# A kernel of two attention layers and two convolutions: the end of the second attention core in halves, fewer row transfers, and other orders of steps

## The chip, the cores and the metric

The kernel runs on one core of a Trainium2 chip. A core has five engines with queues of their own that work in order and meet at semaphores: PE (TensorE, matmul), DVE (VectorE), ACT (ScalarE), POOL (GpSimd) and SP, which here issues most of the DMA transfers. The metric is device time in microseconds (us) of one launch. The median of three runs is compared; a profile of one more execution tells where its time goes.

## The reference, cut to what matters

The input `x` has 2048 rows of 512. Four layers are added to it in turn: A, B, A, B, each on the layer-normalised `x`; both A layers share their weights, and so do both B layers.

```python
def _A_ref(x, wqkv, wo):            # H = 32 heads of 16, window W = 8, dilation 2
    qkv = split_heads(x @ wqkv); q, k, v = qkv[0], qkv[1], qkv[2]
    idx = pos[:, None] - off[None, :]          # off = 0, 2, ..., 14; masked where idx < 0
    logits = einsum("bhsd,bhswd->bhsw", q, kg) * scale
    attn = softmax(logits)
    o = einsum("bhsw,bhswd->bhsd", attn, vg)
    return merge_heads(o) @ wo

def _B_ref(u, ...):                 # K[d, l] = Re sum_n C P dB: a filter of 2048 taps for each channel
    y = irfft(rfft(pad(u)) * rfft(pad(K)))[:L].astype(bfloat16)
    return y + u * Dskip

x = x + _A_ref(_layernorm(x), A_wqkv, A_wo)
x = x + _B_ref(_layernorm(x), ...)
x = x + _A_ref(_layernorm(x), A_wqkv, A_wo)
x = x + _B_ref(_layernorm(x), ...)
```

## The kernel before

Everything stays on one core. `x` lies in SBUF as `x_sb`, 128 partitions by 16 "rows" (row `a` of partition `p` is token `16p + a`) by 512 channels. No scheduler orders the work: each part is a string of one-letter or short steps (`ORDERK`, `CORE0`, `ORDER0`, `ORDERF`, `CORE1`, `ORDER1`), and the engines get their instructions in the order in which the steps stand there. A step issues instructions on several engines at once: a matmul group on PE and its copy out of PSUM on ACT or DVE, for instance. So moving a step in a string moves it in every queue that it uses.

The parts in order of time:

- `k_gen` (`ORDERK`) makes the filters `K`, normalises `x`, and projects the first layer's `k` and part of `q`. It does not change.
- `LayerA.core` (`CORE0`, later `CORE1`) is the attention. `m` multiplies `q` by shifted `k` (DVE, tile `prod`), `l` sums over channels (PE, tile `L` in PSUM), `x`, `e`, `r`, `n`, `T` are the softmax; `P` multiplies attention by shifted `v` for one row (DVE, tile `pav`); `S` (or `V`, with wider matmuls) sums that over the window on PE into `po` and copies it to `oT` (ACT); `O` projects `oT` with `wo` (PE, into a tile `pq` that `p` has filled with the old `x` where it stands ahead) and copies the result to `x_sb` (ACT). `a` and `f` normalise a finished row into `u` for the convolution on DVE and ACT; `b` and `d` begin and end the statistics of a block of four rows. The last row (15) is multiplied in two halves of 256 channels, so that PE can start on the first.
- In `CORE0` more steps are woven in: `1` and `6` load the two halves of the filter rows (`k_load`), `A` to `H` permute them, `W` to `Z` and `2` to `5` make a table of sines, `w` loads a quarter of the table `w_sb`.
- `FftB.run` (`ORDER0`, `ORDER1`) is the convolution through a two-step Fourier transform, for two halves of the channels: `K` and `U` transform filter and input (first step; the letter A or D behind says whether ACT or DVE copies out), `k` and `u` the second step, `m` multiplies spectra (DVE), `y` or `Y` (wider matmuls) is the first inverse step, `w`, `v` and `z` the second one with the addition into `x_sb` for eight rows of 128 channels, four rows of 128, or four rows of 256. In the first convolution each result of `k` is also exchanged between neighbouring partitions by transfers, and stored for the second convolution, which loads it back.
- `ORDERF` is the passage from the first convolution into the second attention: `h`, `H`, `a`, `p`, `n` are statistics, root and normalised rows of four rows at a time, `T` the transposes on PE, `E` their copies out, `P` and `Q` the projections of `k` and `q` (PE, copied by ACT), `x` shifted copies of `k`.

The lines that the argument uses: L342 (`m` of the core), L467 (`P`), L492 and L482 (`S`, `V`), L494 (copy to `oT`), L509 (`O` on PE), L514 (its copy to `x_sb`), L138 (row statistics), L155 and L156 (root as logarithm and exponential on ACT), L195 and L197 (a normalised row on ACT, on DVE or POOL), L811 (copies out of the Fourier steps), L822 (first step on PE), L868 (`m` of the convolution), L880 (copy of `u`), L943 and L944 (second inverse step), L946 and L948 (its addition on DVE, its copy on ACT), L1425 (row transfers of `k_load`), L599 (loads of `w_sb`).

After the string `CORE1` the core's end is written out as plain calls: statistics of rows 12 to 14, projection of row 15, eight matmuls whose result nobody reads, statistics of row 15, and the normalised rows 12, 13 (DVE), 14 (ACT) and 15 (DVE).

## Time and profile before

| what | us |
|---|---|
| median of 3 runs (lowest, highest) | 398.29 (397.69, 398.57) |
| the profiled execution's own time | 398.55 |
| its span, first to last instruction | 396.7 |
| busy in the span: DVE | 377.6 |
| busy in the span: PE (matmul) | 345.0 |
| busy in the span: ACT | 333.1 |
| busy in the span: POOL | 43.3 |

The 1.85 us between the profiled execution's time and its span lie ahead of the first instruction and behind the last. An engine that is busy for most of a stretch sets its length; idle time of another engine in that stretch costs nothing. A row of a timeline has start, duration (of all its instructions, where several are merged), engine, line, operation, tiles and shapes, the count, and in brackets the idle time of the engine before it with what ended it. Durations of neighbouring rows overlap by about 0.1 us. Granted clock of the core over the span: 0.976; it is 1.00 in every stretch from 107 us to 381 us.

### The profile page before, as it was taken

Reading aid. Unit: us, or ns where it says so; the run is one execution under the profiler, and the core shown is the slowest. Engines: PE = TensorE matmul, PEld = TensorE weight load, DVE = VectorE, ACT = ScalarE, POOL = GpSimd, SP = SyncE. Lnnn points to the kernel's source line nnn. Section 1 sums busy time; section 2 is a strip of 40 time slices with the busy share of each in tenths; the row PEclk is TensorE's granted clock in tenths of the full one; section 3 lists DMA queues with packets and bytes.
Section 4 is the critical chain, followed back from the end, with each engine's and each line's share of the span. In section 5 each row is a group of like instructions: output and inputs, shape, how many; then the busy total and the mean of one; then the engine's idle time right before and its main releaser. Section 6 shows DMA issues by size and latency. Waiting matters only on the chain.

```text
span 396.7 us, 14893 instructions
## 1 busy us (share of the span) xinstructions
PE 345.0 (87%) x6509; PEld 236.4 (60%) x6556; DVE 377.6 (95%) x453; ACT 333.1 (84%) x594; POOL 43.3 (11%) x93
## 2 busy tenths in 40 slices
PE   3865768799999999899997879999999998887895
PEld 2221236485645677666886878543456676566885
DVE  6999999999999999999999899979999999989995
ACT  7999999999568789989999987675566889989974
POOL 9400100000370001002422200100000001000000
PEclk9996599999999999999999999999999999999999
DMA  7953610313215756395563744820153029504507
GB/s 215 396 158 47 72 55 10 85 29 79 65 48 143 192 156 192 98 327 208 178 234 130 286 141 111 293 81 0 34 167 93 5 90 338 162 4 144 179 5 214
DMA packets 63695, 54.18 MB, mean 137 GB/s; under 512 B 33033, under 2 KB 49966, under 8 KB 63374
## 3 DMA queue, kind: packets, MB, share of 16 engines
q1 hardware_dynamic: 61958, 48.70, 41.2%
q0 software_dynamic: 1664, 4.52, 3.1%
q8 instruction: 51, 0.84, 0.8%
q14 instruction: 14, 0.11, 0.2%
q10 hardware_dynamic: 8, 0.00, 0.0%
HBM read 30.15 MB, written 13.24 MB: 109 GB/s over the span
## 4 chain that ended last, share of the span: by engine, by line
PE 37%; DVE 27%; ACT 20%; DMA 8%; issue 6%; SPq 1%; POOL 1%; DVEq 0%; ACTq 0%; POOLq 0%
DVE pav L467 7%; PE pq L398 6%; ACT a1s L811 5%; PE pq L223 4%; PE pk L1320 4%; PE pp L282 3%; DVE t L868 3%; DVE prod L342 3%; DMA w_sb<-w_dram 3%; PE pp L1258 2%; PE po L492 2%; ACT ub L880 2%; PE L L350 2%; DVE A_t L1154 2%; DVE ln_bn L138 2%
## 5 line engine op out<-in xcount | busy, mean ns | idle before, releaser
L467 DVE TENSOR_TENSOR pav<-attn,v_ext 128x4096 bf16<-128x4096 bf16 (+1 forms) x34 | 72.0, 2158 | 0.3
L342 DVE TENSOR_TENSOR prod<-qT,kT_ext 128x4096 bf16<-128x4096 bf16 x29 | 65.2, 2283 | 0.7 <-PE L L350 0.5
L1154 DVE TENSOR_TENSOR A_t<-A_t,pow_t 128x1024 bf16<-128x1024 bf16 (+4 forms) x46 | 38.0, 871 | 0.4
L492 PEld LDWEIGHTS <-pav 64*128 64x128 bf16 x1664 | 26.4, 95 | 13.6 <-DVE pav L467 7.1
L880 ACT CAST ub<-pb 128x1024 bf16<-128x1024 f32 x32 | 31.9, 1088 | 2.2 <-DVE t L868 1.2
L509 PE MATMUL pq<-wop,oT 128*128 128x512 bf16 x113 | 30.9, 380 | 3.0 <-issue 1.5
L492 PE MATMUL po<-ident,pav 64*128 64x64 bf16 x1664 | 28.9, 190 | 4.3 <-ACT oT L484 1.8
L829 PE MATMUL pb<-a1s,w_sb 128*128 128x64 bf16 x768 | 27.6, 193 | 5.5 <-ACT ub L880 1.9
L398 PE MATMUL pq<-wv,xnT 128*128 128x512 bf16 x122 | 29.8, 379 | 0.2
L829 PEld LDWEIGHTS <-w_sb 128*128 128x128 bf16 x768 | 24.8, 98 | 8.0 <-issue 6.2
L811 ACT CAST a1s<-pb 128x1024 bf16<-128x1024 f32 x29 | 28.1, 1061 | 1.1 <-PE pb L822 1.1
L400 ACT CAST v_ext<-pq 128x512 bf16<-128x512 f32 x32 | 18.7, 587 | 12.0 <-PE pq L398 11.9
L1258 PE MATMUL pp<-xnT,kT_ext 128*128 128x512 bf16 x88 | 23.0, 379 | 6.3 <-ACT xnT L1251 3.1
L225 ACT CAST qT<-pq 128x512 bf16<-128x512 f32 x24 | 14.0, 585 | 12.8 <-PE pq L223 12.8
L1320 PE MATMUL pk<-B_t,A_t 128*64 128x84 bf16 (+1 forms) x512 | 23.4, 201 | 0.9 <-ACT kgs L1328 0.8
L1320 PEld LDWEIGHTS <-A_t 128*64 128x64 bf16 (+1 forms) x512 | 21.5, 103 | 4.3 <-issue 1.4
L811 DVE CAST a1s<-pb 128x1024 bf16<-128x1024 f32 x19 | 22.5, 1213 | 1.4 <-PE pb L822 1.3
L223 PE MATMUL pq<-xnT,kT_ext 128*128 128x512 bf16 x89 | 23.4, 380 | 0.4
L1122 PE MATMUL pt<-ws,ident 128*128 128x512 f32 x16 | 11.8, 830 | 11.5 <-ACT ws L1109 11.5
L398 PEld LDWEIGHTS <-xnT 128*128 128x128 bf16 x128 | 11.7, 98 | 13.6 <-issue 1.3
L509 PEld LDWEIGHTS <-oT 128*128 128x128 bf16 x128 | 11.5, 98 | 13.1 <-ACT oT L494 2.2
L822 PE MATMUL pb<-F1c,xnT 128*64 128x128 bf16 x256 | 17.3, 219 | 1.6 <-ACT a1s L811 0.6
(279 smaller groups left out, 901.6 us busy)
## 6 DMA issues: line engine op xcount, KB each, us to landing
w_sb<-w_dram SPq DMA_DIRECT2D x32, 256.0 KB, 5.4
w_dram<-xnT SPq DMA_DIRECT2D x1, 4096.0 KB
kf_ring<-kf_dram SPq DMA_DIRECT2D x13, 256.0 KB, 3.9
kf_ring<-kf_dram SPq DMA_DIRECT2D x26, 128.0 KB, 3.5
v_ext<-v_ext SPq DMA_DIRECT2D x4, 784.0 KB, 6.2
x_blk<-in_A_x_dram SPq DMA_DIRECT2D x4, 512.0 KB, 4.7
kT_ext<-in_A_wqkv_dram SPq DMA_DIRECT2D x4, 512.0 KB, 9.7
x_sb<-in_A_x_dram SPq DMA_DIRECT2D x4, 512.0 KB, 7.0
```

Of the source, the lines that this page charges most:

```text
L223: nc.tensor.matmul(pq[:], lhsT=self.wqk[:, dt, ft * P:(ft + 1) * P], rhs=self.xnT[:, dt, q * 512:(q + 1) * 512], start=(dt == 0), stop=(dt ...
L342: nc.vector.tensor_tensor(pr, self.qT[q][:, ft].unsqueeze(1).to_broadcast([P, W, 4, P]), kap, ALU.mult)
L398: nc.tensor.matmul(pp[:], lhsT=xnT[:, dt, a * P:(a + 1) * P], rhs=wv[:, dt, :], start=(dt == 0), stop=(dt == NDT - 1))
L467: nc.vector.tensor_tensor(pv[:, i], attn[:, n % 4].unsqueeze(2).to_broadcast([P, W, DH // parts, H]), vap, ALU.mult)
L492: nc.tensor.matmul(po[:, h, 0, i * nt + ft, :], lhsT=pvf[rows, i, w, ft * P:(ft + 1) * P], rhs=ident[rows, rows], start=(w == 0 and ft + i ...
L509: nc.tensor.matmul(pw[:], lhsT=oT[:, ftp, :], rhs=self.wo[:, ftp, :], start=False, stop=(ftp == NDT - 1), skip_group_check=ahead)
L811: (self.nc.scalar.copy if eng == "act" else self.nc.vector.tensor_copy)(dst, src)
L829: nc.tensor.matmul(p2[:, j, :], lhsT=self.w2[:, ec * EC + j, :], rhs=a1s[:, ec * EC + j, :], start=True, stop=True)
L880: nc.scalar.copy(ub[:], p2)
L1154: return lambda: nc.vector.tensor_tensor(*args)
L1258: nc.tensor.matmul(pps[kind, b, ft][:], lhsT=la.wqk[:, dt, c:c + P], rhs=la.xnT[:, dt, b * 512:(b + 1) * 512], start=(dt == 0), stop=(dt = ...
L1320: nc.tensor.matmul(o, lhsT=lhs, rhs=Bt[:, ri, c * CH + ql].rearrange("p b g -> p (b g)"), start=(not half and j % 4 == 0 and ri == 0), sto ...
```

## The change

Four things are done together.

1. `k_load`: the block of 16 partitions, whose rows repeat with a period, is loaded by four transfers of four rows each instead of nine of one to three rows. This is so for each half of the channels. The bytes written are the same.
2. The end of the second core becomes steps of its string, `A` to `M`: row 15 is summed, copied and projected in two halves (`S` and `K`, then `L` and `M`), the second half in a bank of the tile `L`; the statistics of row 15 (`B`) follow directly; its normalised row (`I`) is taken out of PSUM (`pws[r]`), and its copy to `x_sb` (`D`) comes behind it on ACT. Row 13 is normalised by ACT (`G`) instead of DVE. The eight unread matmuls (`J`) come behind the projection.
3. The strings `CORE0`, `ORDER0`, `ORDERF`, `CORE1` and `ORDER1` are other orders of (nearly) the same steps. In `CORE0` and `CORE1` the letters are the same but for those of item 2; the first 107 letters of `CORE1` are unchanged.
4. In these strings a few copies change engine or width: in `ORDER0` one `UD` becomes `UA`; in `ORDERF` `E20D` becomes `E20A` and `v100A` becomes `v100D`; in `ORDER1` `w011D` becomes `v013A` and `v012D`, `v110A` becomes `v110D`, and one `yA` becomes `YA`.

```diff
 ORDER0 = """
-KD a q KA c3 c1 t s KA KA KD KA g r KD e c2 KA KD KA c6 c0 c5A KD c7 kA kD c4D KA kA kD KA KD UA KD
-UA UA UD KA UD UA UD UA kA kD kA kD u UD u UA UA m UD u u m m u u UA m m u u kD UA UA m m UA kD kA
-kD m u u u kD kD kA kA m m m yA u u YA yD m yA m u u u yA YA yA m m m w000D yD yA YD yA YA yD yA
-w010D
+a KD s t q KA KA KA KD KA c3 KD KA g c2 KD KA r e c0 KD KA c1 c5A c6 c4D c7 kA kD KA KD UA KD UA UA
+UD KA UD UA UD UA kA kD kA kD kA kD u u u m m u kD UA kD m m kA UA UA u UD u u kD UA UA UA UA m m kD
+kD kA u u m m u kA m u m u m yA m u YA yD m u u u m m m yA yA YA yD w000D yA yA YD yA YA yD yA w010D
 """
 ORDERF = """
-yA h00 YA h01 v100A v110D h10 a0 z12A p0 z11A n0D h11 w001A w011A S a1 p1 T0 E01A z13A E00D n1G H2
-P02 a2 P00 Q00 p2 T1 E10D E11D P01 P11 P12 n2D H3 a3 P13 T2 P10 E20D E21D P03 p3 P21 P22 n3D P23 T3
-E30D E31A P20 x1
+h00 yA YA v100D v110D w011A h10 a0 h01 p0 z11A n0D z12A h11 S w001A T0 a1 E01A p1 z13A E00D n1G P03
+H2 Q00 P00 T1 a2 p2 P01 P02 E10D E11D n2D H3 a3 P11 P12 T2 E20A P10 E21D p3 n3D P13 P21 x1 P20 T3
+E31A E30D P22 P23
 """
 ORDER1 = """
-UA UD UA UD UA UA UD UA UD UD u u m m u u m m UA u UA UD m UA u u UD UA u m m u u m m u YD m u YA YA
-m u yD m yA u u m m u w001A m m yA yA w000D YA yD yA YD w011D yA yD w010D yA yD yA v101A v103D v113A
-v102D v112D v111D v110A v100A
+UA UD UA UD UA UA UD UA UD UD u u m u m UA UA UD u u m m UA UD m u m UA u m u u m m u m u u YD YA YA
+m u yD yA yA m m u u w000D m m YA YA u w001A m v013A v012D w010D yD yA YD yA yD yA yD yA v102D v101A
+v111D v103D v113A v112D v110D v100A
 """
 CORE0 = """
-0mvvmlmvxvqllmqemvvrWvXlnmlvvmTvqYxlqlvvvvevvZmmPPllrqxqSqnTemVlmOOPP1Sl5PmSP8Oqm2V4O3PS7llbrOOx
-nVPBeSOPSCd6wOPSwrPPnOSOSPPOSOPSbO9bFwEPAwVGaafOdSttDfOaHafa
+0vvmmlvvqmllxvevvmmrvnllqmmxTqqlvvlXvvmmvvvveqPP1llYZrmWxnqmVqTeSqPPOS5OS2llPOV4OPS8mm3ll7brPOVP
+OSnxPPOOSeBSbrO6PPnSOSOPSOPSPwd9CObaafPdVOFAttwwwfaGSEOHafaD
 """
 CORE1 = """
 0mv12m3llmmqqqlqvlvmmvxvllmvevqrmvnllqqTvvmmlqlxmmvPPvvvvveqlmlqxmqSrnOSTpPPOlSeSrPOSOPSPPOSqlpO
-SpmmOlOplnpPSxPeObbPdrpwVffaSfdOOPnVPPpfSpOSPpObafPSwOtppSdfwafwtaOa
+SpmmOlOplnpbwwPdbfSxefPOdafVpfaPPrnSfOpVOPPSpOwPSpwOfSpbPOtSpdaKfatOLMABCEGaIHDJF
 """
...
+                nt = NDT // parts
+                if l and n == NA - 1:
+                    return last_row(pvf, parts, nt)
...
+            def last_row(pvf, parts, nt):
+                oT = wk.tile([P, NDT, P], BF16, name="oT")
+                last_part(pvf, oT, nt, 0, ps_o.tile([P, 2, 2, NDT, 64], F32, name="po")[:, :, 0])
+                b = self.ps_l.tile([P, W, P], F32, name="L")
+                bank = b[:].rearrange("p (b w) c -> p b (w c)", b=2)[:, :, 0:NDT * 64].rearrange("p b (t q) -> p b t q", q=64)
+                ops["K"] = iter([lambda: last_part(pvf, oT, nt, 1, bank)])
+                ops["L"] = iter([lambda: out_part(pws[NA - 1], oT, 0, nt)])
+                ops["M"] = iter([lambda: out_part(pws[NA - 1], oT, nt, NDT)])
+
+            def last_part(pvf, oT, nt, i, po):
+                for w in range(W):
+                    for ft in range(i * nt, (i + 1) * nt):
+                        for h in range(2):
+                            rows = slice(64 * h, 64 * h + 64)
+                            nc.tensor.matmul(po[:, h, ft, :], lhsT=pvf[rows, i, w, (ft - i * nt) * P:(ft - i * nt + 1) * P], rhs=ident[rows, rows],
+                                             start=(w == 0 and ft == i * nt), stop=(w == W - 1), skip_group_check=True)
+                f = slice(i * nt, (i + 1) * nt)
+                nc.scalar.copy(oT[:, f].rearrange("p t (h q) -> p h t q", h=2), po[:, :, f])
+
+            def out_part(pw, oT, f0, f1):
+                for ftp in range(f0, f1):
+                    nc.tensor.matmul(pw[:], lhsT=oT[:, ftp, :], rhs=self.wo[:, ftp, :], start=False, stop=(ftp == NDT - 1), skip_group_check=True)
...
+                def last_apply():
+                    u_end(r)
+                    ln_apply(nc, u[:, :, r, :], pws[r][:].rearrange("p (q r) -> p q r", r=4), *lns[r], 0, "dve")
+
+                for key, f in dict(A=lambda: u_begin(12, r, "dve", "act"), B=lambda: row_stats(nc, lnst, pws[r][:], r, "dve"),
+                                   C=lambda: u_begin(r, NA, "dve", "act"), D=lambda: nc.scalar.copy(x_sb[:, r, :], pws[r][:]),
+                                   E=lambda: u_end(12), F=lambda: u_apply(12, (12,), "dve"), G=lambda: u_apply(12, (13,), "act"),
+                                   H=lambda: u_apply(12, (14,), "act"), I=last_apply,
+                                   J=lambda: self.warm(pq_tile(), 8, self.wo[:, 0, :])).items():
+                    ops[key] = iter([f])
...
-            u_begin(12, 15, "dve", "act")
-            out_proj(15)
-            pw = pq_tile()
-            self.warm(pw, 8, self.wo[:, 0, :])
-            u_begin(15, 16, "dve", "act")
-            u_end(12)
-            u_apply(12, (12, 13), "dve")
-            u_apply(12, (14,), "act")
-            u_end(15)
-            u_apply(15, (15,), "dve")
...
+        if len(runs) > 2 * s:
+            for c in range(2 * s):
+                t = row[c] // s
+                assert row[c::2 * s] == [row[c] + 2 * s * i for i in range(q // 2)]
+                rows = kd[base + t:base + t + np_ * q, ds_].rearrange("(p i) d -> p i d", i=q)[:, 0::2]
+                nc.sync.dma_start(kr[p0:p1, c::2 * s, :], rows)
+            continue
```

More of the change, by code (lines that the diff above doesn't have):

```diff
@@ L566, in core @@
             ops = {key: iter(f) for key, f in ops.items()}
+            if l:
+                r = NA - 1
+                def last_apply():
[7 more added lines that the diff above has]
+                    ops[key] = iter([f])
             sums, applied = iter(rows), iter(range(12))
```

5 lines of the change are left out of this document (1 added, 4 removed).

## The prediction

> **What bounds the kernel now.** I read first the busy time by stretches, cut at the change's places: 107 to 183 us is the first attention core, 183 to 240 the first convolution (its list of steps `ORDER0`), 240 to 264 the passage `ORDERF`, 264 to 352 the second core, then the second convolution `ORDER1`. Columns: busy us and instructions of PE, PEld, DVE, ACT, POOL, then granted clock, DMA share, GB/s.
>
> ```profile
> core 0: us, PE busy (x) PEld busy (x) DVE busy (x) ACT busy (x) POOL busy (x), PEclk, DMA share, GB/s
> 107.00:183.00 76.00, 72.44 (x1420) 46.41 (x1435) 75.20 (x57) 63.06 (x129) 10.94 (x19) 1.00 0.57 169
> 183.00:231.80 48.80, 41.58 (x1266) 37.52 (x1264) 47.05 (x53) 47.02 (x54) 13.61 (x23) 1.00 0.57 204
> 231.80:240.00 8.20, 7.72 (x240) 7.11 (x241) 7.34 (x10) 6.54 (x8) 0.00 (x0) 1.00 0.24 78
> ...
> 248.70:264.40 15.70, 15.60 (x107) 8.45 (x108) 13.69 (x36) 10.62 (x21) 1.08 (x2) 1.00 0.67 235
> 264.40:345.70 81.30, 76.56 (x1486) 46.40 (x1502) 80.30 (x57) 61.20 (x132) 1.03 (x1) 1.00 0.35 107
> 345.70:352.30 6.60, 5.50 (x98) 3.08 (x92) 5.19 (x17) 5.70 (x13) 0.00 (x0) 1.00 0.08 24
> 352.30:381.20 28.90, 24.47 (x711) 22.68 (x705) 28.73 (x26) 27.92 (x31) 0.00 (x0) 1.00 0.36 112
> ```
>
> DVE sets both cores and the second convolution: idle 0.8, 1.0 and 0.2 us. In the first convolution DVE and ACT are both nearly full (1.75 and 1.78 us idle up to 231.8, then 0.86 and 1.66). From 248.7 to 264.4 PE is full. So no stage can lose work by reordering; what can go is idle time on the list that is full, and that is little. Idle time elsewhere is worth nothing. The sum is made against the profiled execution, 398.55 us, whose span is 396.7; the median of the three timed runs, 398.29, lies 0.26 below it.
>
> **Fewer row transfers, and the first core's order.** Next SP's timeline, and the one place where DVE waits for a transfer near it.
>
> ```profile
> 137.88 14.54 SPq L1425 DMA_DIRECT2D k_rl<-kd_dram  x17
> ...
> 166.51 10.52 SPq L599 DMA_DIRECT2D w_sb<-w_dram  x16
> ```
> ```profile
> 177.59 0.43 DVE L1502 COPY k_perm<-k_rl 128x1024 bf16<-128x1024 bf16 x1 [0.23 <-DMA w_sb<-w_dram]
> ```
>
> Each half of the table loses 5 of its issues; at 14.54/17 = 0.86 us that frees 4.3 us of SP in the first half. The cover is DVE's list, full over the stretch, so the gain lies between 0 and the 0.23 us of that wait: I take 0. The loads of `w_sb` are moved: four issue near DVE's 69th microsecond of the core, twelve five list-microseconds later, 181.5 by my count, and at 10.52/16 = 0.66 us each they are out by 189.4. The first step that uses the table copies out at 191.20 (row in the next part) and needs the first piece alone, so 0; with that cover gone it would be one landing late. The letters of the core's list are the same before and after, so DVE's work is too; its 0.8 us of idle may vanish or double. I take 0, ends -0.8 and +0.8.
>
> **First convolution (`ORDER0`).** The counts of steps differ in one: a copy of the forward transform goes from DVE (`UD`) to ACT (`UA`). The last product (`m`) now stands before the last five inverse steps `y` of the first channel half, which need none of the late products; before it stood behind all of them but one. ACT and DVE timelines, durations in the second column (for a group: all of it):
>
> ```profile
> 191.20 1.01 ACT L811 CAST w_sb<-pb 128x1024 bf16<-128x1024 f32 x1
> ...
> 193.90 6.54 ACT L811 CAST a1s<-pb 128x1024 bf16<-128x1024 f32 x7
> ...
> 228.30 1.01 ACT L880 CAST ub<-pb 128x1024 bf16<-128x1024 f32 x1 [1.17 <-DVE t L868]
> ...
> 232.49 1.01 ACT L811 CAST z<-pb 128x1024 bf16<-128x1024 f32 x1 [0.43 <-PE pb L898]
> 234.06 3.15 ACT L811 CAST z<-pb 128x1024 bf16<-128x1024 f32 x3 [0.56 <-PE pb L898]
> 237.77 2.01 ACT L811 CAST z<-pb 128x1024 bf16<-128x1024 f32 x2 [0.56 <-PE pb L898]
> ```
> ```profile
> 226.99 1.22 DVE L868 TENSOR_TENSOR t<-ub,kn 128x2048 bf16<-128x2048 bf16 x1 [1.43 <-DMA kn<-kn]
> ...
> 229.40 2.35 DVE L868 TENSOR_TENSOR t<-ub,kf_nat 128x2048 bf16<-128x2048 bf16 x2
> ```
>
> ACT gains 6.54/7 = 0.93 us of work. DVE reaches the last product one copy earlier (1.13, as rows of products and copies stand 1.13 to 1.15 apart): 231.75 - 1.13 = 230.6, or 229.2 if the wait of 1.43 goes too (the filter steps `k` stand earlier, so their exchange transfers have longer). After the last `u`, ACT has ten steps `y`, 9.3 us, of which the first four wait for nothing; it comes to the fifth after 230.6, so the three waits for PE, 0.43 + 0.56 + 0.56 = 1.55 us, go. Of the 1.17 and of the small waits ahead I count 0.2 more. The last `y` then ends 0.93 - 1.75 = -0.8 us from its 239.78. Ends: none goes, +0.93; all of ACT's idle goes (1.78 + 1.66 by the stretches), -2.5.
>
> **Passage (`ORDERF`).** What starts the full stretch of PE at 248.75 is the chain from the last `y` through the statistics and normalised rows of the first block.
>
> ```profile
> 241.08 0.67 DVE L946 TENSOR_TENSOR x_sb<-pb,x_sb 128x512 bf16<-128x512 f32 x1
> 241.86 1.41 DVE L150 BATCH_NORM_STATS2 ln_bn<-x_sb 128x6 f32<-128x256 bf16 x4
> 243.18 0.41 DVE L1551 BATCH_NORM_AGGREGATE ln_ag<-ln_bn 128x2 f32<-128x12 f32 x4
> 244.10 0.16 DVE L185 SCALAR_TENSOR_TENSOR ln_nb<-ln_ag,ln_rstd 128x4 f32<-128x4 f32 x1 [0.51 <-ACT ln_rstd L156]
> 244.30 1.38 DVE L197 TENSOR_SCALAR xn<-x_sb,ln_rstd,ln_nb 128x512 bf16<-128x512 bf16 x4
> ...
> 247.24 0.64 DVE L273 COPY xnT<-pt 128x1024 bf16<-128x1024 bf16 x1
> ```
> ```profile
> 247.35 0.21 ACT L155 ACTIVATE ln_rstd<-ln_ag 128x4 f32<-128x4 f32 x1 [0.56 <-DVE ln_ag L1551]
> ...
> 247.70 0.99 ACT L273 COPY xnT<-pt 128x1024 bf16<-128x1024 bf16 x1
> ```
> ```profile
> 248.75 1.46 PE pp L282 x6
> ```
>
> Before: 248.75 - 239.78 = 8.97 us. After, on DVE: 0.5 for PE's first piece, two adds from PSUM 1.3 (one was ACT's), statistics 1.3, sums 0.35, four more statistics 1.35 (they now cover the 0.51 of the square root, but stand in the chain), the rows 1.5, statistics and sums of the next block 1.7, the copy 0.65: 8.65. ACT's copy of 0.99 stood behind the second root and thereby behind DVE's second sums; now it stands ahead of it and is done before DVE's. So -0.3. Ends: if only ACT's order counts, 248.75 - 247.93 = -0.8; if the add and the four statistics cost all their time less the 0.51, 0.65 + 1.35 - 0.51 = +1.5. Beyond it PE is full to 264.4, then DVE: the shift is passed on. The third block's copy that goes from DVE to ACT is off that path, 0; if PE should wait for it, the 0.35 by which ACT's copy is longer than DVE's.
>
> **Second core's end.** The list up to the last row's products has the same letters: 0, ends -1.0 and +1.0 (its idle). Then the part that the change names:
>
> ```profile
> 343.31 2.36 DVE L467 TENSOR_TENSOR pav<-attn,v_ext 128x2048 bf16<-128x2048 bf16 x2
> ...
> 348.76 0.66 DVE L138 BATCH_NORM_STATS2 ln_bn<-pq 128x6 f32<-128x512 f32 x1
> ...
> 350.61 0.42 DVE L197 TENSOR_SCALAR xnT<-x_sb,ln_rstd,ln_nb 128x512 bf16<-128x512 bf16 x1
> ```
> ```profile
> 347.04 1.53 ACT L195 ACTIVATE xnT<-x_sb,ln_nb,ln_rstd 128x512 bf16<-128x512 bf16 x2
> ...
> 349.46 0.59 ACT L514 CAST x_sb<-pq 128x512 bf16<-128x512 f32 x1
> ...
> 350.18 0.20 ACT L156 ACTIVATE ln_rstd<-ln_rstd 128x1 f32<-128x1 f32 x1
> 350.29 0.80 ACT L195 ACTIVATE xnT<-x_sb,ln_nb,ln_rstd 128x512 bf16<-128x512 bf16 x1
> ```
> ```profile
> 351.18 0.22 PE L822 MATMUL pb<-F1c,xnT 128*64 128x128 bf16 x1 [0.20 <-ACT xnT L195]
> ```
>
> From the end of the products, 345.67, to the last normalised row, 351.03, DVE has work without a gap: four statistics, three rows of the third block, sums, rows 12, 13, 15. Halving the sums and the projection shortens the chain products, sums, copy, projection by about 0.8 us, but the last statistics wait for DVE's own list, not for it: 0; with the cover gone, as late as before. What counts is the list: row 13 goes to ACT (-0.35), row 15 is read from PSUM. Its price is not in the trace; bounds 0.42 (from SBUF) and 0.66 (statistics from PSUM, same 512 elements), taken 0.65 for the same source. DVE then ends at 350.95. On ACT the copy of 0.59 no longer stands ahead of the second root, which ends near 349.85 instead of 350.38; but two rows stand behind it, 1.53 as in the pair at 347.04: 351.4. The first transform waits for both engines: 351.5 against 351.18, +0.3. Ends: -0.3 (the 0.53 of the root, less what DVE doesn't follow), +0.8 (one ACT row in full).
> The Trainium skill, page "VectorE: DVE Perf Modes", section "Mode 2×_2P", says that PSUM has one read port for this engine, so the doubled modes are out: against this edit. Its clock of 0.96 GHz would make an estimate of 512/0.96 = 0.53 us for the row; with it DVE ends at 350.85 and the sum stays, since ACT is later. The statistics read from PSUM, 0.66 for the same 512 elements, agree with one element a cycle and a fixed part.
>
> **Second convolution (`ORDER1`).** The same work on DVE, but a full store step (`w000D`, 1.13 us) now precedes the last product, and the eight small steps that end the kernel hold five for DVE and three for ACT, instead of four and four.
>
> ```profile
> 375.43 5.75 DVE L868 TENSOR_TENSOR t<-ub,kf_ring 128x2048 bf16<-128x2048 bf16 x5
> ...
> 390.57 1.89 DVE L946 TENSOR_TENSOR x_sb<-pb,x_sb 128x512 bf16<-128x512 f32 x3 [0.44 <-PE pb L944]
> ```
> ```profile
> 375.88 3.00 ACT L880 CAST ub<-pb 128x1024 bf16<-128x1024 f32 x3
> ...
> 392.14 1.26 ACT L948 CAST x_sb<-pb 128x512 bf16<-128x512 f32 x2 [1.42 <-PE pb L944]
> ```
>
> The last product ended at 381.18. After, DVE's list brings it to 381.18 + 1.13 + 0.3 = 382.6; but three more `y` stand ahead of the last `u` on ACT, 378.88 + 2.8 + 0.3 = 382.0, less whatever ACT catches up, so it ends near 383.0. Then DVE has 0.6 + 1.13 + 4 x 1.13 + 5 x 0.6 = 9.3 us, to 392.3, and PE and ACT end one small step behind, 392.95, against 393.40. With the 0.3 from above that is -0.75 for this part. Ends: -1.4 (ACT's last wait) and +0.3 (the late `u` costs another product's 1.13 and nothing but DVE's 0.44 and small waits come back). The stores are the same eight.
>
> **Sum.** -0.8 - 0.3 + 0.3 - 0.75 = -1.55 us: 398.55 - 1.55 = 397.0 us.
>
> **Rivals.** (1) The change doesn't save what its order says: the exchange transfers still hold DVE at 1.43 us, and only 0.9 of ACT's waits goes, so the first convolution gives 0; with -0.3, +0.3 and -0.5 (a third of the last part's gain taken back by the late `u`) the time is 398.05. For it: those transfers are bound by DMA traffic, which the order only spreads. Against: the filter steps stand some 5 us of list earlier. Chance 0.20.
> (2) ACT becomes the bound, and it is slower. ACT gets 0.93 us in the first convolution, a row at the second core's end and three early `y` in the second. If its waits only move, the last `y` is +0.93, the passage's DVE chain grows by 0.5, the core's end by 0.4, and -0.75 remains: +1.1, 399.6. It decides once less than 0.9 us of the 3.4 goes. For it: ACT idles 1.78 of 48.8 us there, as little as DVE. Against: 1.55 of the waits are for PE steps that no longer hang on a late product. Chance 0.24.
> (3) All those waits go (-2.5) and the small steps end by their best: 394.9. It is the far end of the forecast's own case.
>
> **Numbers.** Forecast 0.56: 397.0, its own range 394.9 to 397.7. About 0.2%, 0.8 us, is what a measurement of this kernel can tell from no change. Faster 0.56, same 0.20 (rival 1), slower 0.24 (rival 2). To hold 8 in 10 the range takes in rival 1 and rival 2 to its price: 394.9 to 399.7.
>
> **What would show it.** In the changed profile: ACT's last `z` copy of the first convolution near 239.0 with the waits for PE gone; DVE's wait for `kn` gone; PE's full stretch starting near 247.6; the first transform of the second convolution following the last ACT row, 5.7 us after the last product pair; DVE without a gap from 352 to 392. It is wrong if ACT's waits reappear ahead of the `u` copies, if PE's stretch starts later than 248.75, or if the products of either core wait.

## The result, and the profile after

The change makes the kernel slower. Twelve runs of the changed kernel have a median of 401.69 us (400.54 to 405.92), twelve of the kernel before on the same chip 399.40; the ratio over all the runs is 1.0069, 95% interval 1.0046 to 1.0092 (the two medians alone give 1.0057). The profiled execution took 401.82 us, its span 400.0: 3.3 us more than before. Forecast were 397.0 us.

The profile after is cut at the events that end each stage: the first product of the first core, the end of its last product of attention and `v`, the end of ACT's last `z` copy, the start of PE's full stretch in the passage, the first product of the second core, its last product, the first transform of the second convolution, and the end of the last copy. Columns as in the prediction's first view.

```profile
core 0: us, PE busy (x) PEld busy (x) DVE busy (x) ACT busy (x) POOL busy (x), PEclk, DMA share, GB/s
106.58:182.45 75.87, 71.60 (x1364) 44.25 (x1363) 73.28 (x52) 59.57 (x123) 13.36 (x20) 1.00 0.57 167
182.45:241.73 59.28, 52.62 (x1573) 46.48 (x1571) 56.81 (x67) 57.76 (x67) 14.40 (x23) 1.00 0.52 181
241.73:249.87 8.14, 8.09 (x108) 7.54 (x108) 7.88 (x28) 5.45 (x9) 0.00 (x0) 1.00 0.55 134
249.87:266.04 16.17, 16.17 (x111) 8.69 (x110) 13.83 (x37) 11.78 (x23) 1.68 (x2) 1.00 0.66 227
266.04:348.00 81.96, 78.51 (x1491) 46.59 (x1491) 80.14 (x56) 61.12 (x130) 2.94 (x1) 0.98 0.33 104
348.00:353.79 5.79, 4.73 (x74) 2.22 (x67) 5.43 (x17) 5.52 (x16) 0.00 (x0) 1.00 0.17 54
353.79:396.62 42.83, 37.45 (x1080) 35.11 (x1080) 39.46 (x37) 36.27 (x41) 0.00 (x0) 1.00 0.36 112
```

The same stages of the kernel before take 73.75, 59.50, 8.97, 15.70, 81.22, 5.51 and 42.22 us (its events: 106.53, 180.28, 239.78, 248.75, 264.45, 345.67, 351.18, 393.40). So 2.12 us of the loss lie in the first core, 0.74 in the second, 0.28 in its end, 0.61 in the second convolution; the first convolution and the passage give back 0.22 and 0.36.

In the first core DVE's work is nearly the same (73.28 us against 72.95, by the same cut of the kernel before); it idles, 2.59 us against 0.80. The timeline of DVE in the changed kernel shows where: ahead of the steps `b`, whose first two instructions (L169, L171) need ACT's sums of a row that has just been projected.

```profile
154.34 0.16 DVE L169 SCALAR_TENSOR_TENSOR ln_msq<-ln_s 128x4 f32<-128x4 f32 x1 [0.67 <-ACT x_sb L540]
155.10 0.16 DVE L171 SCALAR_TENSOR_TENSOR ln_veps<-ln_s,ln_msq 128x4 f32<-128x4 f32 x1 [0.59 <-ACT ln_junk L144]
...
178.61 0.16 DVE L169 SCALAR_TENSOR_TENSOR ln_msq<-ln_s 128x4 f32<-128x4 f32 x1 [0.21 <-ACT x_sb L540]
179.37 0.16 DVE L171 SCALAR_TENSOR_TENSOR ln_veps<-ln_s,ln_msq 128x4 f32<-128x4 f32 x1 [0.59 <-ACT ln_junk L144]
```

Those are 2.06 us. ACT in turn waited for PE's projection, and PE, in the timeline of PE, for nothing that the profile shows ("issue"), between the first and the second of four matmuls of one projection; two smaller such pauses, 0.58 and 0.79 us, stand at 145.54 and 149.54, ahead of the first of these `b`.

```profile
173.79 1.11 PE L493 MATMUL po<-ident,pav 64*128 64x64 bf16 x64
174.83 0.39 PE L531 MATMUL pq<-x_sb,ident 128*128 128x512 bf16 x1
175.06 0.38 PE L533 MATMUL pq<-wop,oT 128*128 128x512 bf16 x1
177.03 0.82 PE L533 MATMUL pq<-wop,oT 128*128 128x512 bf16 x3 [1.59 <-issue]
```

The page of the changed kernel says what it may have waited for: one DMA queue carries instructions.

```profile
PE 351.0 (88%) x6536; PEld 237.1 (59%) x6536; DVE 377.8 (94%) x452; ACT 335.2 (84%) x597; POOL 48.0 (12%) x93
...
q8 instruction: 51, 0.84, 0.9%
```

PE has 6536 matmuls and as many weight loads, 13,072 instructions; 51 packets of 0.84 MB together are 16.5 KB each, one for 256 instructions. So PE's list comes in pieces of 256 through the same DMA engines that load the tables. In narrow cuts of the DMA view such a packet starts at 174.43 us, and PE goes on at 177.03, 2.60 us later; in the same way 171.80 and 174.08 in the kernel before, 2.28 us, where the pause is 0.23. When the packet started, PE had some 42 instructions left in the changed kernel and some 135 in the kernel before. At 174 to 175 us the loads of `w_sb` fill the queues (387 GB/s in that microsecond). The Trainium skill, page "Runtime: NRT & Kernel Launch", section "Instruction fetch mechanics", describes blocks of 16 KiB or 256 instructions, which the sequencer fetches by a DMA queue of its own, and calls the cost of crossing a block's end mostly hidden. The size agrees with this trace; the hiding does not, with 1.59 us.

The other stages, first convolution and passage (ACT, then DVE):

```profile
235.97 3.08 ACT L838 CAST z<-pb 128x1024 bf16<-128x1024 f32 x3 [0.48 <-PE pb L925]
239.61 2.12 ACT L838 CAST z<-pb 128x1024 bf16<-128x1024 f32 x2 [0.56 <-PE pb L925]
```
```profile
224.62 2.35 DVE L895 TENSOR_TENSOR t<-ub,kn 128x2048 bf16<-128x2048 bf16 x2
...
235.39 1.23 DVE L838 CAST z<-pb 128x1024 bf16<-128x1024 f32 x1 [0.47 <-PE pb L921]
237.57 1.23 DVE L838 CAST z<-pb 128x1024 bf16<-128x1024 f32 x1 [0.95 <-PE pb L925]
...
264.85 0.69 DVE L294 COPY kT_ext<-kT_ext 128x2032 bf16<-128x2032 bf16 x1 [1.76 <-ACT kT_ext L284]
...
329.03 0.16 DVE L184 SCALAR_TENSOR_TENSOR ln_nb<-ln_s,ln_rstd 128x4 f32<-128x4 f32 x1 [0.93 <-POOL ln_rstd L177]
...
352.51 0.81 DVE L196 TENSOR_SCALAR xnT<-pq,ln_rstd,ln_nb 128x512 bf16<-128x512 f32 x1
...
393.36 1.29 DVE L973 TENSOR_TENSOR x_sb<-pb,x_sb 128x512 bf16<-128x512 f32 x2 [0.92 <-PE pb L971]
```

In the kernel before DVE's wait at those steps was one:

```profile
235.73 1.22 DVE L811 CAST z<-pb 128x1024 bf16<-128x1024 f32 x1 [0.59 <-PE pb L898]
```

DVE's wait for `kn` (1.43 us before) is gone. Of ACT's three waits for PE near the end two are left (1.55 us before, 1.04 now), but DVE's own waits for the same steps have grown from 0.59 to 0.47 + 0.95 us. The second core has one new wait, 0.93 for POOL, told of below. The row out of PSUM takes 0.81 us.

### The profile page after: what moved, and what is told of

It is laid out like the page before. It is cut to its first block, busy times and chain, and to the rows that moved or that the text cites. A ratio compares the mean times of both kernels' runs of the same rounds, so it can differ in the third digit from the quotient of the medians.

```text
span 400.0 us, 14890 instructions
## 1 busy us (share of the span) xinstructions
PE 351.0 (88%) x6536; PEld 237.1 (59%) x6536; DVE 377.8 (94%) x452; ACT 335.2 (84%) x597; POOL 48.0 (12%) x93
## 4 chain that ended last, share of the span: by engine, by line
PE 47%; DVE 18%; ACT 18%; issue 8%; DMA 5%; SPq 1%; POOLq 1%; POOL 1%; DVEq 0%; ACTq 0%
PE pq L397 7%; DVE pav L466 6%; ACT a1s L838 4%; PE pp L281 4%; PE pk L1347 3%; PE pq L222 3%; PE pq L533 3%; PE pp L1285 3%; PE po L493 2%; PE pb L921 2%; DVE t L895 2%; DVE prod L341 2%; PE L L349 2%; PE pb L925 2%; DVE A_t L1181 2%
## 5 line engine op out<-in xcount | busy, mean ns | idle before, releaser
L533 PE MATMUL pq<-wop,oT 128*128 128x512 bf16 x124 | 33.1, 388 | 2.6 <-issue 2.4
L493 PEld LDWEIGHTS <-pav 64*128 64x128 bf16 x1600 | 25.4, 95 | 12.8 <-DVE pav L466 6.5
L838 ACT CAST a1s<-pb 128x1024 bf16<-128x1024 f32 x30 | 29.1, 1044 | 0.6 <-PE pb L849 0.5
L1285 PE MATMUL pp<-xnT,kT_ext 128*128 128x512 bf16 x96 | 24.1, 380 | 5.4 <-ACT xnT L1278 2.9
L838 DVE CAST a1s<-pb 128x1024 bf16<-128x1024 f32 x18 | 21.3, 1213 | 1.6 <-PE pb L849 1.5
L540 ACT ACTIVATE x_sb<-pq 128x512 bf16<-128x512 f32 x24 | 14.2, 593 | 7.1 <-PE pq L533 7.0
```

What stands on the lines that cost most here:

```text
L493: nc.tensor.matmul(po[:, h, 0, i * nt + ft, :], lhsT=pvf[rows, i, w, ft * P:(ft + 1) * P], rhs=ident[rows, rows], start=(w == 0 and ft + i ...
L533: nc.tensor.matmul(pw[:], lhsT=oT[:, ftp, :], rhs=self.wo[:, ftp, :], start=False, stop=(ftp == NDT - 1), skip_group_check=ahead)
L838: (self.nc.scalar.copy if eng == "act" else self.nc.vector.tensor_copy)(dst, src)
L1285: nc.tensor.matmul(pps[kind, b, ft][:], lhsT=la.wqk[:, dt, c:c + P], rhs=la.xnT[:, dt, b * 512:(b + 1) * 512], start=(dt == 0), stop=(dt = ...
```

## The experiments

All kernels start from the kernel before or the changed one; ratios are to the kernel before on the same chip, with 95% intervals. The table holds the stages of each profiled execution, cut by the same events; "passage" runs from ACT's last `z` copy to the first product of the second core.

| kernel | first core | first conv. | passage | second core | its end | second conv. | ratio |
|---|---|---|---|---|---|---|---|
| before | 73.75 | 59.50 | 24.67 | 81.22 | 5.51 | 42.22 | 1 |
| changed | 75.87 | 59.28 | 24.31 | 81.96 | 5.79 | 42.83 | 1.0069 (1.0046 to 1.0092) |
| p1_core0 | 76.42 | 60.14 | 24.67 | 81.26 | 5.51 | 42.32 | 1.0061 (1.0035 to 1.0088) |
| p1_conv0 | 73.76 | 62.32 | 24.32 | 81.43 | 5.51 | 42.25 | 0.9999 (0.9980 to 1.0019) |
| p1_core1 | 73.75 | 60.36 | 24.66 | 82.23 | 5.79 | 42.48 | 1.0022 (0.9997 to 1.0048) |
| p1_order1 | 73.77 | 60.14 | 24.67 | 81.21 | 5.51 | 42.39 | 0.9991 (0.9967 to 1.0015) |
| p2_b_late | 76.42 | 61.55 | 24.32 | 82.45 | 5.83 | 41.86 | 1.0065 (1.0030 to 1.0099) |
| p2_rows_old | 75.92 | 59.77 | 24.31 | 82.55 | 5.95 | 42.41 | 1.0030 (1.0001 to 1.0059) |
| p2_w_split | 75.16 | 59.45 | 24.31 | 82.48 | 5.81 | 42.35 | 1.0060 (1.0022 to 1.0098) |
| p2_shift | 73.83 | 59.52 | 24.31 | 81.96 | 5.64 | 42.88 | 1.0033 (1.0008 to 1.0058) |
| p3_shift_before | 73.76 | 59.86 | 24.67 | 81.22 | 5.51 | 42.24 | 0.9982 (0.9959 to 1.0006) |
| p3_shift_d | 74.00 | 60.03 | 24.32 | 81.74 | 5.83 | 42.89 | 1.0016 (0.9994 to 1.0038) |
| p3_shift_d2 | 74.34 | 60.05 | 24.32 | 81.73 | 5.85 | 43.25 | 1.0015 (0.9994 to 1.0036) |
| p4_after_2shift | 73.83 | 59.55 | 24.32 | 81.95 | 5.65 | 42.08 | 1.0018 (0.9999 to 1.0037) |
| p4_best | 74.95 | 60.28 | 24.32 | 81.21 | 5.51 | 42.03 | 0.9993 (0.9969 to 1.0016) |

Each row is a single execution. That of p1_conv0 was the slowest of its twelve (401.14 us), that of p2_b_late 1.8 us above its median.

**One part at a time.** Four kernels take one part of the change each: `CORE0` with the row transfers, `ORDER0` with `ORDERF`, `CORE1` with its new end, and `ORDER1`.

> The kernel before with only the new order of the first core and the fewer row transfers. Theory A (the new order puts the steps that begin a block's statistics, `b`, right behind the projection of the block's last row, so DVE stands behind ACT's copies and sums, 0.67 + 0.59 + 0.21 + 0.59 us in the changed trace): first core's last product of attention and v ends near 182.4 instead of 180.3, and the time rises by 2.1 to 2.9 us (ratio 1.005 to 1.007). Theory B (the first core is slower in the changed kernel only because of what stands behind it, the new start of the first convolution): no more than +0.8 us (1.002).

> The kernel before with only the new orders of the first convolution and of the passage. By the places of the changed trace the convolution gains 0.9 and the passage 0.9, and 0.55 of it is lost again where the second core's first product waits for the last key projections (ACT copies kT_ext): -1.2 us (ratio 0.997). The rival, that the orders of convolution and first core only fit together: no gain, 0 or slower (1.000 to 1.005).

> The kernel before with only the new order of the second core and its new end (last row in halves, taken out of PSUM). By the places of the changed trace: +0.75 inside the core (DVE waits 0.93 for POOL's power ahead of the first block's end) and +0.3 at its end: +1.05 us (ratio 1.0026). The prediction's own step: +0.3 (1.0008). The rival, that the wait only shows since the core starts late: 0 or less.

> The kernel before with only the new order of the second convolution. By the changed trace PE, not DVE, sets the last eight microseconds, and the order loses 0.4 to 0.6 us (ratio 1.001 to 1.0015). The prediction's step: -0.75 us (0.998). The rival, that the loss belongs to the late last rows of the second core: 0.

The four ratios add up to +0.73%, the whole change costs 0.69%: the parts are nearly independent. The first core's part is the only one whose interval lies off 1: +0.61%, 2.67 us in its own stage (0.55 more than in the whole change; the granted clock fell to 0.72 for some 6 us near 150 us in this execution). The second core with its end costs what the changed trace showed (1.01 + 0.28 us; the timed ratio alone could be 1). The convolution and passage gain nothing by themselves: their trace has a PE pause of 1.34 us at 237.40 and 1.67 us more between the last product of the core and DVE's first copy (5.81 against 4.14). In that stretch DVE's normalised rows run beside POOL's (POOL starts on them at 182.66 there, at 185.97 in the kernel before), and the last two take 1.57 us instead of 0.73; why is not tested. `ORDER1` alone loses 0.17 us in its stage, with a PE pause of 0.68 us in the last microseconds; its forecast was -0.75.

**Where does the first core lose: the places of `b`, or PE?** Theory A: `b` stands too early. Theory C: PE is late because its instructions are, and `b` only hands that on. Four kernels, all the changed one with an edit.

```diff
 CORE0, p2_b_late: each b one or two products later
-...ll7brPOVP...eBSbrO6PPnS...CObaafPdV...
+...ll7rPbOVP...eBSrO6PPbnS...COaafPbdV...
 CORE0, p2_w_split: half of the table's loads ahead of the second row transfers
-...rO6PP...Attwwwf...
+...rOww6PP...Attwf...
 p2_rows_old: k_load as in the kernel before
 k_gen, p2_shift: in a gap of PE near 9 us
+        pw = pst.tile([P, 4, P], F32, name="pt")
+        for _ in range(32):
+            nc.tensor.matmul(pw[:, 0, 0:4], lhsT=ident[:], rhs=ident[:, 0:4], start=True, stop=True)
```

> The changed kernel with three letters of the first core moved back: each `b` (beginning of a block's statistics on DVE) one or two products later than now; nothing else. Theory A (the places of `b` cost the first core's 2.1 us): DVE's waits for x_sb and ln_junk ahead of L169 and L171 (0.67 + 0.59 + 0.21 + 0.59 us) go, the core's DVE stretch from first product to last product of attention and v falls from 75.87 to about 73.9 us, and the time by 1.5 to 2.0 us (ratio to before 1.002 to 1.003). Theory C (PE is late, since it ran out of instructions for 0.8 and 1.6 us, and only hands its lateness on through `b`): the DVE stretch shortens too, but DVE or ACT then wait for PE's last projections in the first convolution's start, and the time falls by less than 0.8 us (ratio 1.005 or more).

> The changed kernel with the row transfers of before (nine short ones instead of four of four rows, in each half). Theory C1 (the shorter list lets the loads of the table w_sb run at full DMA rate earlier, and PE's instruction pieces, which come over the same DMA engines, come late): PE's pause for nothing shown at 177.0 shrinks from 1.59 to below 0.9 us, and the core's DVE stretch by about 0.8 us. Theory A: the pause may change, DVE's waits at `b` stay, 75.9 us.

> The changed kernel with half of the loads of the table w_sb ahead of the second half's row transfers, so that the burst of sixteen is cut into two of eight. Theory C: PE's pause at 177.0 shrinks by half or more (1.59 to 0.8 or less), and DVE's last wait at `b` (0.80 us) shrinks with it; the risk is a later k_rl, 0 to 2 us. Theory A: no effect on the first wait at `b` (154 us), and at most 0.8 us on the last.

> The changed kernel with 32 tiny matmuls more near 9 us, whose result nobody reads, in a gap of 1.3 us of PE; all later PE instructions are the same but stand 64 places further in PE's list. Theory C (PE's list comes in pieces of 256 instructions over DMA): the pauses for nothing shown move by 64 places; that at 177.0 is no longer behind the first matmul of a projection but 32 matmuls earlier, inside the sums ahead of it. If the pauses belong to the instruction where they stand, they stay at that projection. For the time: within 1 us of the changed kernel, with either sign.

`p2_shift` decides. It leaves every step of the order where it is and moves only where the pieces of PE's list end, and the first core takes 73.83 us, as before. Its whole list of DVE waits from 107 to 183 us is the first line, with none at `b`; of PE's waits for instructions the second line is the longest entry. Its five are not even pauses: each is 0.16 us, and in front of each the trace has no record of the matmul with the old `x` (L531, 14 recorded of 21) that the code puts there.

```profile
DVE prod L341 <- ACT qT L224: 0.3, 1, 0.3
...
PE pq L533 <- issue: 0.8, 5, 0.2
```

Three later kernels have the same first core with the same shift, and in them the pause is seen where theory C puts it, behind 34 of the 64 sums (this is `p3_shift_d2`):

```profile
171.93 0.67 PE L493 MATMUL po<-ident,pav 64*128 64x64 bf16 x34
173.83 0.61 PE L493 MATMUL po<-ident,pav 64*128 64x64 bf16 x30 [1.23 <-issue]
```

It lasts 0.90 us in `p3_shift_d`, 1.23 in `p3_shift_d2` and 0.62 in `p4_after_2shift`, and their first cores take 74.00, 74.34 and 73.83 us. Without the shift the changed kernel, `p1_core0`, `p2_rows_old` and `p2_b_late` take 75.87 to 76.42. In timed runs `p2_shift` alone is not clear of the changed kernel (1.0008 to 1.0058 against 1.0046 to 1.0092); `p4_after_2shift` is (0.9999 to 1.0037).

So the places of `b` cost nothing as long as PE is on time, and A as I put it falls. `p2_w_split` comes at it from the other side: the pieces end where they did, but DMA is less crowded (199 GB/s in the microsecond in which the packet starts, 387 in the changed kernel), the pause at 177 us shrinks to about 0.2 us, the last wait at `b` (0.80 us) goes, and the stage falls to 75.16 us; the first wait stays (0.52 + 0.59), with pauses of 0.94 and 0.51 ahead of it. C's forecast held for the place that the edit touches. Its timed runs scatter too widely (399.84 to 405.75) to show 0.7 us. `p2_rows_old` was a miss for C1: the pause at 176.2 is 1.59 us as in the changed kernel, so the row transfers aren't its cause. Its timed ratio is lower than the changed kernel's, but the intervals overlap and the stage is the same. `p2_b_late` came out at C's ratio, but the shorter stage that both theories forecast did not come (76.42 us), and its profile is no clean proof: PE's granted clock fell in it, columns as above,

```profile
148.00:151.00 3.00, 2.41 (x34) 1.19 (x32) 3.00 (x3) 1.23 (x2) 0.00 (x0) 0.79 0.60 163
151.00:154.00 3.00, 3.00 (x35) 2.88 (x34) 2.98 (x3) 1.46 (x5) 0.00 (x0) 0.64 0.60 189
```

behind a PE pause of 1.25 us at 145.9, and DVE then waits for PE's sums in other places.

A crowded DMA can't be the whole reason for a late piece. The same `p2_w_split` has a pause of 0.46 us in its second core. The piece's packet starts at 309.88 us and is all that DMA moves from 307 to 312 us (the microsecond with its start, columns as above, and PE's timeline):

```profile
309.00:310.00 1.00, 1.00 (x66) 0.95 (x66) 1.00 (x1) 0.85 (x4) 0.00 (x0) 1.00 0.06 16
...
312.25 0.21 PE L493 MATMUL po<-ident,pav 64*128 64x64 bf16 x3 [0.46 <-issue]
```

The 1.34 us in `p1_conv0` came with 17 GB/s. In all pauses over 0.3 us behind 100 us PE goes on 2.2 to 3.2 us behind the packet's start, whether DMA is full or empty. What differs is how much PE has left when the packet starts: some 127 instructions here, some 42 in the changed kernel at 174.43, 5 in `p2_rows_old`. In a run of sums PE gets through 128 instructions in 1.11 us (the row at 173.79), so none of these is enough. Whether full DMA queues delay the start was not tested by itself.

**Why the kernel before is spared.** The same 32 matmuls in the kernel before:

> The kernel before with the same 32 tiny unread matmuls near 9 us as in p2_shift, nothing else. Theory C (in the changed kernel a piece of PE's list ended by chance right behind the sums of a row, where PE runs through its list fastest; in the kernel before the same place was covered, since PE waited for DVE's products there): the small pause behind the first matmul of a projection near 174 us (0.2 to 0.8 us) moves 64 places ahead, no DVE wait comes or goes, and the time is that of before within 0.2% (0.998 to 1.002). If shifting by itself makes a kernel faster (as a warmer PE, or a later start of something), it gains 1.0 to 1.5 us (0.997) as the changed kernel did.

```profile
172.42 0.67 PE L492 MATMUL po<-ident,pav 64*128 64x64 bf16 x34
173.68 0.61 PE L492 MATMUL po<-ident,pav 64*128 64x64 bf16 x30 [0.59 <-issue]
```

As expected: the pause has moved from behind the first matmul of the projection to 30 sums, one residual matmul and one projection matmul ahead of it, 32 matmuls and their weight loads, exactly the 64 places. No wait of DVE came or went, and the time is that of before. What spares it is the lead that PE and ACT have over DVE. At the first `b`, ACT's last sum and DVE's instruction that needs it, in the kernel before:

```profile
153.78 0.19 ACT L145 ACTIVATION_READ_ACCUMULATOR ln_junk<-x_sb 128x1 f32 x1
...
155.98 0.16 DVE L172 SCALAR_TENSOR_TENSOR ln_veps<-ln_s,ln_msq 128x4 f32<-128x4 f32 x1
```

and in `p2_shift`, the new order with PE on time:

```profile
153.23 0.18 ACT L144 ACTIVATION_READ_ACCUMULATOR ln_junk<-x_sb 128x1 f32 x1
...
153.67 0.16 DVE L171 SCALAR_TENSOR_TENSOR ln_veps<-ln_s,ln_msq 128x4 f32<-128x4 f32 x1
```

2.0 us of lead against 0.26. (At the first instruction of this `b`, L170 and L169, it is 1.77 against 0.01.) The new order has used up the lead; any lateness of PE beyond it reaches DVE. At the last `b` the leads are alike (0.8 and 1.0 us), and there it is the size of the pause, 1.59 us, that goes through.

**The second core and the tail.** Two kernels with the 32 matmuls; the second also moves the tail against the pieces.

```diff
 CORE1, p3_shift_d and p3_shift_d2
-...bwwPdbfSxefPOdaf...
+...bwwPbSxePdffOdaf...
 core, p3_shift_d2 only
-J=lambda: self.warm(pq_tile(), 8, self.wo[:, 0, :])
+J=lambda: self.warm(pq_tile()[:, 0:4], 40, self.wo[:, 0, 0:4])
```

> The changed kernel with the 32 matmuls and, in the second core's string, the first two `d` one product later (the letters `d` and `f` behind them move by one `P`). The wait of DVE for POOL's power at L184 (0.93 us; POOL's power takes 2.94 us beside a product of DVE, 1.03 us between two) goes, so the second core's DVE stretch falls from 81.96 to about 81.2 us, and the time by 0.7 us against p2_shift (ratio 1.0015 where that had 1.0033). The rival, that DVE or ACT then wait for something else (ACT's normalised rows come 2.3 us later): no gain, 81.9 us.

> As p3_shift_d, and the eight unread matmuls of 512 columns at the second core's end are forty of 4 columns, so PE's list of the second convolution stands 64 places further against the pieces. Theory C: the pause of 1.22 us near 389 us moves by 64 places and, as p2_shift showed, need not come back as long; the last stretch, from the first transform to the end, falls from 42.9 to about 42.0 us, and the time lies at that of before (ratio 0.998 to 1.0005). If the new order of the second convolution is slow by itself: 42.9 us stay. A risk: forty small matmuls keep PE 0.3 us longer ahead of the first transform.

The wait of 0.93 us in the second core comes from POOL, whose power of 128 x 4 numbers takes 2.94 us in the changed kernel and 1.03 in the kernel before. Their POOL timelines, each with the product of DVE that runs beside it:

```profile
326.06 2.94 POOL L177 TENSOR_TENSOR ln_rstd<-ln_rstd,ln_mh 128x4 f32<-128x4 f32 x1 [74.05 <-DVE ln_rstd L176]
...
325.82 2.28 DVE L466 TENSOR_TENSOR pav<-attn,v_ext 128x4096 bf16<-128x4096 bf16 x1
```
```profile
330.12 1.03 POOL L178 TENSOR_TENSOR ln_rstd<-ln_rstd,ln_mh 128x4 f32<-128x4 f32 x1 [80.34 <-DVE ln_msq L170]
...
330.26 2.28 DVE L467 TENSOR_TENSOR pav<-attn,v_ext 128x4096 bf16<-128x4096 bf16 x1
```

Before, a second `b` stands between the first and the next product, and the power starts 0.14 us ahead of that product; now the product follows at once, the power starts 0.24 us behind its start and ends 0.90 us behind its end. So it is not "beside a product" against "between two", as the expectation has it: in both kernels the power overlaps one, and what differs is which starts first. It is 2.94 us in all nine traces where the product does, 1.03 in the six where the power does. The Trainium skill, page "SBUF — State Buffer", section "SBUF: two separate sides", says that DVE and GpSimd share a pair of ports as an exclusive lock, held for a whole instruction by whichever starts first. The changed kernel agrees: a power that can only work from the product's end on needs 0.90 us there, near its 1.03. The other way round the trace does not show it, since the product behind the power takes 2.28 us as ever. `p3_shift_d` removes the wait, but only 0.22 of the 0.74 us come back, since DVE then waits elsewhere: the rival held.

```profile
335.85 0.69 DVE L447 TENSOR_TENSOR attn<-ex,rs 128x1024 bf16<-128x1024 bf16 x1 [0.66 <-ACT rs L439]
```

`p3_shift_d2` took the pause out of the tail and lost more ahead of it. Forty matmuls of 4 columns don't keep PE's clock up as eight of 512 do; the granted clock, third number from the right, is 0.80, 0.50, 0.84 (1.00 in the kernel before and in `p3_shift_d`):

```profile
352.00:354.00 2.00, 1.76 (x51) 1.79 (x53) 0.73 (x2) 1.61 (x3) 0.00 (x0) 0.80 0.00 0
354.00:356.00 2.00, 2.00 (x43) 2.00 (x41) 1.46 (x2) 1.10 (x2) 0.00 (x0) 0.50 0.04 8
356.00:358.00 2.00, 2.00 (x67) 2.00 (x64) 1.13 (x2) 2.00 (x3) 0.00 (x0) 0.84 0.00 0
```

So it could not tell what the order of the second convolution is worth. The next one keeps the columns (40 of 104 for 8 of 512) and the 64 places, with the second core of the change; and a last kernel takes the change without its second core, with both moves.

```diff
+J=lambda: self.warm(pq_tile()[:, 0:104], 40, self.wo[:, 0, 0:104])
```

> The changed kernel with the 32 tiny matmuls near 9 us, and the eight unread matmuls of 512 columns at the second core's end replaced by forty of 104 columns: 64 more places in PE's list, the same columns. If the pause is what the second convolution lost: no pause over 0.5 us behind 380 us, granted clock 1.00 from 352 to 358 us, and from the first transform to the end 41.5 to 42.0 us (42.88 with the pause of 1.22 us, 42.22 in the kernel before); time 0.9 us below p2_shift (ratio about 1.001). If the order is slow by itself: 42.8 us or more. If the clock falls again (0.5 to 0.8 in those rows), the test fails and the time is that of p3_shift_d2 (43.2 us).

> The kernel before with the change's row transfers, first core, both orders of the first convolution and passage and second convolution, without its second core and end, and with the same two moves of PE's list (32 tiny matmuls; eight unread matmuls turned into forty of 104 columns). By the stages measured without pauses: first core 0, first convolution 0 to -0.5, passage -0.35, second core and end 0, second convolution -0.2 to -0.7: -0.6 to -1.5 us against before (ratio 0.996 to 0.9985). If the orders are worth nothing even without pauses: 1.000.

```profile
351.80:393.88 42.08, 37.21 (x1080) 35.07 (x1080) 39.46 (x37) 36.24 (x41) 0.00 (x0) 1.00 0.36 114
```

With the pause reduced to 0.4 us the second convolution takes 42.08 us: 0.80 less than with 1.22, and 0.14 less than in the kernel before. It missed the expected 41.5 to 42.0 narrowly; the pause was most of what was lost. `p2_b_late` has the same order and no pause over 0.15 us in this stage, at a clock of 1.00: 41.86 us. So by this one execution the order itself is worth 0.36 us, half of the 0.75, and a pause eats it. The whole changed kernel comes to 1.0018 instead of 1.0069.

`p4_best` is not measurably faster than the kernel before: 0.9993. Its first core took 74.95 us although PE had no pause over 0.5 us: this time the clock fell, and through the small lead it reached DVE at another `b`.

```profile
155.00:157.00 2.00, 2.00 (x8) 0.90 (x7) 2.00 (x2) 1.18 (x4) 1.54 (x1) 0.50 0.61 197
```
```profile
164.50 0.16 DVE L169 SCALAR_TENSOR_TENSOR ln_msq<-ln_s 128x4 f32<-128x4 f32 x1 [0.54 <-ACT x_sb L515]
```

No version beats both kernels by what can be measured.

## Why the prediction was wrong

| term of the sum | forecast | changed kernel | p4_after_2shift |
|---|---|---|---|
| first core and row transfers | 0 | +2.12 | +0.08 |
| first convolution | -0.8 | -0.22 | +0.05 |
| passage | -0.3 | -0.36 | -0.35 |
| second core | 0 | +0.74 | +0.73 |
| its end | +0.3 | +0.28 | +0.14 |
| second convolution | -0.75 | +0.61 | -0.14 |
| sum | -1.55 | +3.17 | +0.51 |

The step that failed is the first core: "The letters of the core's list are the same before and after, so DVE's work is too; its 0.8 us of idle may vanish or double. I take 0, ends -0.8 and +0.8." The work is the same. But the step took DVE's full list for a bound that no order could lengthen, and counted idle time only as something to lose. A full list is full because its suppliers are ahead, by 2.0 us at the first `b`, and an order can spend that lead. The prediction looked at no supplier's lead, and not at PE's pauses for instructions, which stood in the trace of before (0.23 us at 174.08, 0.42 at 224.35). The same step put twelve loads of `w_sb` at 181.5 us, where their letters stand; in fact SP issued all sixteen from 165.88 on, as before from 166.51: they follow the same row transfers in SP's queue, and no row of its timeline shows a wait at their places. So in both kernels they fill DMA at 174 us.

**Second core, "the same letters: 0".** The same fault: the letters are the same, but the pair `b` `b` was separated, and POOL's power fell beside a product: +0.74.

**Second convolution, -0.75.** The last product came where forecast: 31.5 us behind the first transform by the prediction, 31.32 in `p4_after_2shift`. What failed is the sum behind it, "9.3 us" of DVE's work: measured 10.36 (383.12 to 393.48), since the small steps behind the last `z` wait for PE (0.35 and 0.28 us on DVE, 1.01 and 0.98 on ACT). They do so in `p2_b_late` without a pause too (0.41 and 0.28, 1.30 and 0.98). DVE's work was taken for the bound where PE is; the pause adds the rest.

**First convolution, -0.8.** The wait for `kn` went, as forecast, and the three waits of ACT became two; but DVE's waits for the same PE steps grew from 0.59 to 1.42 us. Over the eight profiles with the new order of the convolution behind the new core, `p2_b_late` left out, it takes 59.74 us on average, over the four with both old ones 59.97: -0.2, no more than these profiles scatter (59.28 to 60.28, 59.50 to 60.36).

**Passage and end: right.** In the kernel before PE halts behind the first matmul of the first projection, and its full stretch was counted from behind that halt:

```profile
247.93 0.38 PE L282 MATMUL pp<-xnT,kT_ext 128*128 128x512 bf16 x1
248.75 1.46 PE L282 MATMUL pp<-xnT,kT_ext 128*128 128x512 bf16 x6 [0.45 <-ACT xnT L273]
```

The first projection starts 8.15 us behind ACT's last `z` copy before and 8.14 in the changed kernel; what went is the halt for ACT's copy, as forecast (the stretch, 16.17 us, is 0.47 longer only by the count from 248.75). With two projections of `k` behind the last transposes DVE waits 1.76 us for ACT at the passage's end, 0.35 before. The end cost 0.28 us for 0.3 forecast, with the two rows of ACT setting it as the prediction had it; the row out of PSUM took 0.81 us where 0.65 was taken, and was covered.

A sum of the prediction is off beside this: the terms of its third rival, -2.5, -0.3, +0.3 and -1.4, give 394.65, not 394.9.

None of the rivals was this one. The first (exchange transfers still hold DVE) and the second (ACT becomes the bound) both stayed inside the lists of DVE and ACT; the missing rival was "PE, which looks idle, is late". The falsifier "if the products of either core wait" came nearest: the waits stand at the `b` ahead of the products.

How far the proof goes: that the pauses are moved by where the list's pieces end, and that with them the loss goes, is shown. That a piece comes late because the table's loads are ahead of it in DMA is not: `p2_w_split` fits it for one pause, and other pauses came with DMA nearly idle. What sets the start of a packet stays open, and so does why a pause at the same place lasts 0.62 us in one execution and 1.23 in another. Why the clock fell at 148 to 157 us in some executions (p1_core0, p2_b_late, p4_best) stays open.

## What to carry to other kernels

An engine whose list is full is fed by others; before reordering its steps, measure at each place where it needs a result how long that result has been ready, and count a step that spends this lead as a cost with PE's worst pause as its price. A long pause of PE "for issue" in or behind a run of many tiny matmuls was here the end of a piece of its instruction list: 32 tiny matmuls in an idle gap far ahead moved such a pause and took 2 us off its stage, so a comparison of two orders should be made with more than one such offset. Moving a step in a string moves a DMA only if its queue waits there or if the order within that queue changes: twelve loads of `w_sb` stayed where they were, and the eight that `p2_w_split` put ahead of row transfers came at 156.49 us.

## What the hardware showed that I had not expected

- PE's instructions come in pieces of 256 by DMA, and PE stands still at some pieces' ends, for up to 1.59 us; it goes on 2.2 to 3.2 us behind the start of the piece's packet (171.80 to 174.08, 174.43 to 177.03), with DMA full or nearly idle.
- Forty matmuls of 4 columns in place of eight of 512 let the granted clock fall to 0.80, 0.50 and 0.84 in three stretches of 2 us. The Trainium skill, page "TensorE: Matmul & The Clock Gate", section "Part 1: The HAM clock gate (the "warmup" mystery)", says that the gate goes by how busy PE has been lately; PE was busy 1.43 of the 3 us ahead, against 2.10 in `p3_shift_d` and 2.20 in `p4_after_2shift`, where the clock stayed at 1.00; that fits, but at what share the clock falls no run shows.
- A power of 128 x 4 numbers on POOL took 2.94 us when a product of DVE had started 0.24 us ahead of it, and 1.03 us when it started 0.14 us ahead of the product.
- A normalised row of 512 read from PSUM took 0.81 us on DVE, against 0.42 from SBUF. The clock that the Trainium skill gives for this engine (page "VectorE: DVE Perf Modes", section "Specifications") had given an estimate of 0.53 in the prediction; the measurement decides.
